# Gates folded into the output weights, q placed by DMA, another order of heads and of first loads, in a fused attention and MLP block

## The chip, the core and the metric

The kernel runs on one core of a Trainium2 chip. The metric is device time in microseconds (us); less is better. The engines named below are PE (matrix products, with PEld for its weight loads), DVE (vector), ACT (activation functions), POOL (GpSimd) and SP, which here only starts DMAs. "Idle" is always the idle time of the engine named.

## What is computed

One transformer block with adaptive layer norm, on 2048 tokens of width 512, 32 heads of 16, an MLP of width 1376, all bfloat16:

```python
mod = (silu(c) @ w_mod).reshape(1, 6, 1, 512)
sa, ca, ga, sb, cb, gb = mod[:, 0], mod[:, 1], mod[:, 2], mod[:, 3], mod[:, 4], mod[:, 5]
h = layernorm(x) * (1 + ca) + sa
q, k, v = heads(h @ wqkv)                       # 32 heads of 16
o = softmax(q @ k.T * 0.25) @ v
x = x + ga * (o @ wo)
h = layernorm(x) * (1 + cb) + sb
x = x + gb * (gelu(h @ w1 + b1) @ w2 + b2)
```

`c` has 512 numbers. The gates `ga` and `gb` are vectors of 512, one number for each output column.

## The kernel before

**A planner writes the order.** The code describes operations (`Op`, with engine, estimated time, dependencies, priority) to a small planner (`Plan`), which simulates the engines and emits the instructions of every engine in the order in which it picks them. The order is fixed when the program is built; on the chip each engine runs its own list from the front, waiting on semaphores. Dependencies given to the planner only shape that order; real waits come from the data.

**Tiling.** Tokens are cut into 4 query blocks of 512 and 16 key tiles of 128; the 32 heads stand as 4 column groups `cc` of 128 columns (8 heads of 16). A *run* is one block with half a column group, 4 heads; there are 32 runs, in the order of `runs` (before: block by block, `u` = 0 to 7). One *unit* is the scores of 128 keys by 512 queries of one head: a matmul on 32 rows of PE (L757). Each head of 16 shares its 32 rows with a neighbour, so q is kept as a tile `qm` of two halves in which the other head's rows are zero.

**Two ways to the exponential.** On the A path ACT takes scores out of PSUM, 3 units and 2 units in turn, with Exp (L806, `pt<-st`). On the D path DVE makes an approximate exponential of 4 units out of five shifted integer conversions: 4 instructions L847 (`ph<-ax`) and 4 L862 (`sh<-ph`). Of the 16 key tiles of a run up to 4 may go to D; the planner decides how many, by the time it thinks each engine has. 32 x 16 x 4 = 2048 units in all; before, 1584 go to ACT and 464 to DVE. PE then multiplies by v (L895).

**The start.** SP issues the loads in one queue: x's first block in four pieces, two pieces of `w_mod` for the first modulation (L480, tiles `blk`), then Wk, Wq, Wv and more of x. ACT's queue loads c (L470) as 128 partitions of 4 numbers. DVE normalises x's first block (L564 statistics, L575), PE makes the modulation columns (L539), transposes the normalised block (L612), DVE and ACT modulate it (L583, L580), then PE projects q, k (L649) and v (L678) for the first column group, and the first scores go to ACT. Blocks 1 to 3 follow the same way, each one's K being needed before ACT can go on past the keys of the blocks before it.

**q.** For every later group of heads (15 of them) `make_q` projects 128 columns and one DVE instruction (L667) reads the PSUM result twice, multiplies by a mask that holds the scale and zero, and writes both halves of `qm`. Four `qm` buffers rotate.

**The tails.** `block_tail` (L1077 on) runs for each block after its heads: PE multiplies by Wo (L1045), DVE multiplies the PSUM result by `ga_bc`, the gate spread over all partitions (L1095, `y<-ax,ga_bc`), and adds x (L1097); a second layer norm, W1, gelu and W2 follow, then again a gate (L1146) and an addition (L1149), and the store. The last block's second half has the same pair in `last_half` (L1203 and L1206, L1250 and L1253).

**GpSimd** computes small powers for the layer norms, scaled copies of v (L694) and the normalised attention output (L947); the last are placed by `beside`, which lays each 0.68 us piece next to a DVE instruction that the planner expects not to share a port with it. SP also carries, for each run, a chain of small DMAs through DRAM that spreads the softmax sums (L926, L928, L936, L941, L957).

Of the kernel before, what the change touches and what calls it, by code (L numbers as in the profile page):

```python
# [53 lines left out]
PEL = 0.24  # L54
# [48 lines left out]
class Plan:  # L103
    SLACK = {"NIL": 0.0, "PE": 0.10, "DVE": 0.05, "ACT": 0.15, "POOL": 0.05, "SP": 0.05}

    def __init__(self, dyn, later):
# [4 lines left out]
        self.bus = 0.0  # L111
# [65 lines left out]
    def commit(self, s, o):  # L177
# [36 lines left out]
        if o.kb:  # L214
            self.bus = max(self.bus, s + o.us + 0.9) + o.kb / 260.0
            o.end = self.bus + 0.7
# [13 lines left out]
    def step(self):  # L230
# [6 lines left out]
        if h is not None:  # L237
            hs = max(self.start(h), self.cool)
            end = hs + h.us + 0.11
            if hs <= nxt and (not pe or pe[0][0] >= end or pe[0][1].kind == "qkD" and hs >= self.cool):  # L240
                self.commit(hs, self.add(h))
                if h.acq is not None:
                    h.acq.free[h.slot] = h.end
                return True
# [5 lines left out]
def kernel(  # L250
# [69 lines left out]
    r_qm = res("qm", 4, [P, 2, QB], BF16)  # L320
# [4 lines left out]
    r_y = res("y", 2, [P, D], BF16)  # L325
# [81 lines left out]
    def dma(fn, deps=(), kb=64, eng="SP", n=1, **k):  # L407
        o = op(eng, fn, 0.45 * n if eng == "SP" else 0.1, deps, **k)
# [9 lines left out]
    def heat():  # L418
        if o_warm.end is None or plan.now > plan.until:
            return None  # L420
        if min(r_ax.free) <= max(plan.now, plan.cool):
# [3 lines left out]
        r = pv_run[0]  # L425
        if r is None or left[r] == 0:
# [10 lines left out]
    plan.heat = heat if True else None  # L437
# [7 lines left out]
    c_bf = const.tile([P, NC], BF16, name="c_bf")  # L445
    ce = const.tile([P, NC], FP32, name="ce")
# [23 lines left out]
    o_c = dma(lambda o: nc.scalar.dma_start(out=c_bf, in_=c.rearrange("o (j p) -> p (o j)", p=P)),  # L470
# [15 lines left out]
    o_wm = {i: load_w(wm_src[:, :, i * D:(i + 1) * D], r_blk, prio=0.1) for i in (0, 1)}  # L486
    o_w = {}
    for n, i in enumerate((1, 0, 2)):
        o_w[i] = load_w(wq_src[:, :, i * D:(i + 1) * D], r_w, prio=(0.2, 0.3, 0.5)[n])
    for b in range(1, NQ):  # L490
        o_x[b] = load_x(b)
        o_x[b].prio = 0.4 if b == 1 else b
# [37 lines left out]
    def silu(o):  # L530
        nc.vector.tensor_scalar(out=ce, in0=ce, scalar1=1.0, scalar2=None, op0=ALU.add)
        nc.vector.reciprocal(out=ce, in_=ce)
        nc.vector.tensor_tensor(out=sc, in0=c_bf, in1=ce, op=ALU.mult)
    o_sc = op("DVE", silu, 0.3, (o_ce,), prio=0.0)

    def mod_mm(ps, n, w, m):
# [4 lines left out]
        if m % 2:  # L541
# [3 lines left out]
    def mod_columns(dst, ws, kind):  # L545
        mm = chain([(lambda ps, n=n, w=w, m=m: mod_mm(ps, n, w[1](), m), 0.36)
# [4 lines left out]
        def out_(o):  # L551
# [3 lines left out]
        return op("DVE", out_, 0.3, (mm,), prio=0.0, rel=(mm,))  # L555
    urgent.add("modA")
    o_mA = mod_columns(modA, [(o_wm[i], lambda i=i: o_wm[i].tile, o_wm[i]) for i in range(2)],
                       "modA")
# [33 lines left out]
    def layer_norm(src, deps, mod, mod_dep, hold_z, alloc_h, engines, ps_res, kind, prio,  # L592
# [3 lines left out]
        st = [op("DVE", lambda o, t=t: stats(ln, t, src(t)), 0.83, (deps[t], ln, after), prio=prio)  # L596
# [9 lines left out]
        if isinstance(ps_res, tuple):  # L606
            for half in range(2):
                def tr(o, half=half):
                    o.ps = o.tile.bitcast(BF16)
                    for j in (2 * half, 2 * half + 1):  # L610
                        for t in range(TPB):
                            nc.tensor.transpose(  # L612
                                out=o.ps[:, (j % 2) * QB + t * P:(j % 2) * QB + (t + 1) * P],
                                in_=z.tile[:, t, j * P:(j + 1) * P], identity=ident)
                one = op("PE", tr, 8 * 0.0705, za + [o_id], lat=PEL, mode=("full", 0), kind=kind,
                         acq=ps_res[half], rel=(z,))
                trs.append(one)
                for j in (2 * half, 2 * half + 1):
# [3 lines left out]
                        0.7, (one, mod_dep, h), prio=0.2, rel=(one,)))  # L622
# [25 lines left out]
    def proj(b, w, cc, kind, acq, after=None):  # L648
# [3 lines left out]
            [w, after] + o_hd[b], kind, acq, (o_h[b], w))  # L652

    def make_k(b, cc, kind, acq, eng, after=None):
        mm = proj(b, o_w[1], cc, kind, acq, after)
        o_k[(cc, b)] = op(eng, lambda o: copy(eng, kT[cc][b], mm.tile[:, 0:QB]), 0.6 if eng == 'DVE' else 0.5, (mm,), prio=0.3,
                          rel=(mm,))

    def make_q(b, cc, kind, acq):
# [6 lines left out]
        else:  # L666
            evs = 2 * [op("DVE", lambda o: nc.vector.tensor_tensor(  # L667
                out=qm.tile, in0=mm.tile[:, 0:QB].unsqueeze(1).to_broadcast([P, 2, QB]),
# [724 lines left out]
```

The softmax here doesn't subtract the row's maximum and nothing guards it: scores larger than these inputs give would overflow.

## Time and profile before

| what | value |
|---|---|
| seven runs | 793.02, 793.47, 794.97, 797.55, 797.68, 798.32, 798.80 us |
| median | 797.55 us |
| profiled execution, one of the seven | 793.47 us |
| its span in the trace | 791.7 us |
| PE, DVE, ACT, POOL busy | 728.6, 737.0, 761.8, 100.4 us |
| L806, Exp on ACT | 634 instructions, 719.5 us |
| DMA over the span | 26.22 MB, mean 33 GB/s |
| first Exp starts / last Exp ends | 17.64 us / 766.18 us |

The busy time of a group counts overlapping instructions once, so the 634 Exps take 719.5 us although one of them is under way for 1309 ns on average: the next starts before the last is quite finished. The 1.8 us between span and run time lie outside the trace.

### The profile page before, as it was taken

What the parts mean: (1) busy time and instruction counts of PE and PEld (TensorE: products, weight loads), DVE (VectorE), ACT (ScalarE), POOL (GpSimd) and SP (SyncE); (2) the same over time, 40 slices, a digit from 0 to 9 for tenths busy, and PEclk for the clock granted to TensorE, in tenths of its full rate; (3) what the DMA queues carried; (4) which work ended last, traced back from release to release, by engine and by line L of the source; (5) the groups of instructions that cost most, each with busy time, mean ns of one, the idle gap of its engine ahead of it and who ended that gap; (6) DMA issues with size and microseconds to landing.
All of it is one profiled execution on the core that took longest, in us unless ns stands there. A gap on an engine that the chain in (4) does not pass through costs nothing.

```text
span 791.7 us, 20215 instructions
## 1 busy us (share of the span) xinstructions
PE 728.6 (92%) x8181; PEld 275.3 (35%) x8260; DVE 737.0 (93%) x1292; ACT 761.8 (96%) x691; POOL 100.4 (13%) x237
## 2 busy tenths in 40 slices
PE   7799998999899899989999899999999899999997
PEld 3433333332232233222222323323234443444454
DVE  6878888999999999989999999999999999999974
ACT  2899999999999999999999999999999999999993
POOL 4612312100001100000001000000000100001100
PEclk8999999999999999999999999999999999999999
DMA  6314000102100000001100000001010000100110
GB/s 212 108 32 108 18 17 16 28 21 72 42 19 16 20 15 17 19 8 30 52 19 16 16 19 3 19 16 32 23 49 19 5 18 17 46 18 17 31 44 27
DMA packets 34199, 26.22 MB, mean 33 GB/s; under 512 B 15005, under 2 KB 29502, under 8 KB 34106
## 3 DMA queue, kind: packets, MB, share of 16 engines
q1 hardware_dynamic: 33578, 24.94, 11.1%
q8 instruction: 64, 1.05, 0.5%
q14 instruction: 29, 0.24, 0.1%
q10 hardware_dynamic: 528, 0.00, 0.0%
HBM read 21.30 MB, written 2.61 MB: 30 GB/s over the span
## 4 chain that ended last, share of the span: by engine, by line
ACT 39%; PE 33%; DVE 15%; issue 12%; DMA 1%; SPq 0%; POOLq 0%; POOL 0%; ACTq 0%; DVEq 0%
ACT pt L806 38%; PE od L895 11%; PE st L757 9%; DVE ph L847 6%; DVE sh L862 5%; PE ax L1051 3%; PE ax L757 2%; PE ax L1114 2%; PE ax L649 1%; DMA blk<-in_w_mod_dram 1%; DVE g L1124 1%; ACT g L1133 1%; PE ax L1045 1%; DVE OD L920 1%; PE t L1051 1%
## 5 line engine op out<-in xcount | busy, mean ns | idle before, releaser
L806 ACT ACTIVATE pt<-st 128x1536 bf16<-128x1536 f32 x634 | 719.5, 1309 | 2.6 <-PE st L757 1.9
L847 DVE TENSOR_SCALAR ph<-ax 128x512 int16<-128x512 f32 x464 | 303.2, 685 | 15.3 <-PE ax L757 13.4
L862 DVE TENSOR_SCALAR sh<-ph 128x2048 int16<-128x2048 int16 x464 | 300.3, 693 | 0.3 <-PE od L895 0.2
L757 PE MATMUL st<-qm,kT 32*128 32x512 bf16 x1584 | 248.0, 382 | 33.6 <-ACT pt L806 25.9
L757 PEld LDWEIGHTS <-kT 32*128 32x128 bf16 x2048 | 83.3, 91 | 247.2 <-issue 235.5
L895 PE MATMUL od<-sh,VX 128*32 128x512 bf16 (+1 forms) x2336 | 164.5, 340 | 4.7 <-DVE sh L862 3.6
L757 PE MATMUL ax<-qm,kT 32*128 32x512 bf16 x464 | 160.9, 379 | 5.4 <-DVE ph L847 2.5
L895 PE MATMUL od<-pt,VEB 128*32 128x512 bf16 (+1 forms) x1976 | 145.0, 340 | 0.7 <-DVE OD L920 0.4
L895 PEld LDWEIGHTS <-VEB 128*32 128x32 bf16 x2560 | 62.2, 96 | 74.5 <-issue 60.2
L895 PEld LDWEIGHTS <-VX 128*32 128x32 bf16 x2336 | 56.9, 95 | 84.2 <-issue 73.5
L947 POOL TENSOR_TENSOR OT<-OD,RB 128x256 bf16<-128x256 f32 x38 | 27.9, 745 | 312.6 <-DVE sh L862 177.8
L895 PE MATMUL od<-ph,VEB 128*32 128x512 bf16 (+1 forms) x584 | 45.6, 338 | 0.3 <-DVE OD L920 0.2
L947 POOL TENSOR_TENSOR OS<-OD,RB 128x256 bf16<-128x256 f32 x24 | 17.2, 726 | 176.9 <-DVE sh L862 172.6
L1114 PE MATMUL ax<-blk,W 128*128 128x512 bf16 (+1 forms) x126 | 36.5, 368 | 2.1 <-issue 1.0
L649 PE MATMUL ax<-blk,w 128*128 128x512 bf16 x95 | 31.9, 391 | 2.8 <-issue 1.0
L694 POOL TENSOR_SCALAR VX<-VEB 128x128 bf16<-128x128 bf16 x64 | 24.1, 376 | 69.6 <-DVE VEB L590 58.0
L1051 PE MATMUL ax<-w,g 128*128 128x512 bf16 x101 | 28.2, 381 | 2.0 <-DVE ph L847 1.5
L1124 DVE TENSOR_SCALAR g<-ax,b1c 128x512 bf16<-128x512 f32 (+1 forms) x37 | 26.3, 715 | 0.3 <-PE ax L1114 0.2
L564 DVE BATCH_NORM_STATS2 ln_s<-xb 128x6 f32<-128x512 bf16 x32 | 21.8, 681 | 0.8 <-DMA xb<-in_A_x_dram 0.7
L1051 PEld LDWEIGHTS <-g 128*128 128x128 bf16 x176 | 14.7, 97 | 22.5 <-issue 9.3
L920 DVE COPY OD<-od 128x512 f32<-128x512 f32 x31 | 21.2, 685 | 0.2
L1114 PEld LDWEIGHTS <-W 128*128 128x128 bf16 x176 | 14.2, 97 | 20.6 <-issue 13.6
(107 smaller groups left out, 368.5 us busy)
## 6 DMA issues: line engine op xcount, KB each, us to landing
RB<-rn SPq DMA_DIRECT2D x124, 64.0 KB
xb<-in_A_x_dram SPq DMA_DIRECT2D x8, 512.0 KB
out_dram<-o SPq DMA_DIRECT2D x16, 128.0 KB
w<-in_A_wqkv_dram SPq DMA_DIRECT2D x3, 512.0 KB
W<-in_B_w_dram SPq DMA_DIRECT2D x1, 1376.0 KB
blk<-in_w_mod_dram SPq DMA_DIRECT2D x2, 512.0 KB
g<-in_w_mod_dram SPq DMA_DIRECT2D x2, 512.0 KB
xb<-in_w_mod_dram SPq DMA_DIRECT2D x2, 512.0 KB
```

The source lines that it names most:

```text
L649: return chain([(lambda ps, j=j: nc.tensor.matmul(out=ps[:, 0:QB], lhsT=w.tile[:, j, cc * P:(cc + 1) * P], rhs=o_h[b].tile[:, j, :], start ...
L694: nc.gpsimd.tensor_scalar(out=v_cols(VX[(t, ph)])[:, 8 * cc:8 * cc + 8, 0:16], in0=v_cols(v_tile(t, 0))[:, 8 * cc:8 * cc + 8, 0:16], scala ...
L757: nc.tensor.matmul(out=o.tile[:, k * QB:(k + 1) * QB], lhsT=kT[cc][kb][rows, ko * P:(ko + 1) * P], rhs=qm.tile[rows, par, :] if hb is None ...
L806: nc.scalar.activation(out=e.tile[:, 0:len(got) * QB], in_=o.tile[:, 0:len(got) * QB], func=ACT.Exp, scale=ESC)
L847: nc.vector.tensor_scalar(out=ph.tile[:, o.row * QB:(o.row + 1) * QB], in0=o.tile, scalar1=PH_B, scalar2=0.0, op0=ALU.add, op1=ALU.max)
L862: sh = op("DVE", lambda o, j=j: nc.vector.tensor_scalar(out=o.tile, in0=first.tile, scalar1=PH_SH[j], scalar2=None, op0=ALU.add), 0.6, es, ...
L895: nc.tensor.matmul(out=o_od[r].tile[32 * i:32 * i + 32, n * HB:n * HB + w], lhsT=v_tile(kt, ph)[:, c0:c0 + 32], rhs=got[i][:, at:at + w], ...
L920: OD = op("DVE", lambda o: nc.vector.tensor_copy(out=o.tile, in_=od.tile), 0.6, (last,), prio=0.0, acq=r_OD, rel=(od,))
L947: two = beside(lambda c: nc.gpsimd.tensor_tensor(out=OT.tile[:, c], in0=OD.tile[:, c], in1=o5.tile[:, c], op=ALU.mult), (OT,), (OD, o5))
L1051: nc.tensor.matmul(out=ps, lhsT=g[:, f, col:col + P], rhs=rhs, start=(f == 0), stop=(f == NF - 1))
L1114: mm = chain([(lambda ps, f=f, j=j: nc.tensor.matmul(out=ps[:, 0:N], lhsT=W1[:, j, f * P:(f + 1) * P], rhs=h.tile[:, j, 0:N], start=(j == ...
L1124: ev.append(op("DVE", lambda o, f=f, mm=mm: nc.vector.tensor_scalar(out=g.tile[:, f, 0:N], in0=mm.tile[:, 0:N], scalar1=b1c[:, f:f + 1], s ...
```

## The change

- **c by rows.** c is loaded as 4 partitions of 128; silu works on that, PE transposes the result (one 128x4 matmul) and ACT copies it to `sc`.
- **First loads.** The two `w_mod` pieces are issued from ACT's queue, the second after the first small Exp; SP issues Wq, Wk, Wv, then x of blocks 1, 2, 3. PE's warm-up matmuls (on zeros) now also use the bank `od`, and the planner no longer spaces them before the first scores. Block 0's transposes come in two parts; its four modulations alternate DVE and ACT; its projections start on each modulated quarter as it comes.
- **Gates.** After `Wo` and `ga_bc` are there, POOL multiplies Wo (and `WoP`, the copy for the last half) by `ga_bc` in place: 12 pieces of 128x256. The same for W2 with `gb_bc`: 22 pieces. The tails then only add: one DVE instruction reads PSUM and x.
- **q.** One DVE instruction scales the projection into a tile `qs`, 128x512; eight DMAs of 16 partitions, issued from SP, place it into `qm`. POOL zeroes three `qm` tiles at the start. The first group keeps the mask.
- **Order of heads.** After block 0's first column group come block 1's first, block 0's second and block 1's second, then the rest as before; the due times of the K and V projections follow.

```diff
-    o_c = ... c.rearrange("o (j p) -> p (o j)", p=P)
+    o_c = ... c.rearrange("o (j p) -> (o j) p", p=P)
...
-    o_wm = {i: load_w(wm_src[:, :, i * D:(i + 1) * D], r_blk, prio=0.1) for i in (0, 1)}
+    o_wm = {i: dma(lambda o, i=i: nc.scalar.dma_start(out=o.tile, in_=wm_src[:, :, i * D:(i + 1) * D]),
+                   eng="ACT", kb=512, acq=r_blk, prio=0.0, gate=lambda i=i: i == 0 or o_ce.end is not None)
+            for i in (0, 1)}
...
-    for n, i in enumerate((1, 0, 2)):
-        o_w[i] = load_w(wq_src[:, :, i * D:(i + 1) * D], r_w, prio=(0.2, 0.3, 0.5)[n])
+    for n, i in enumerate((0, 1, 2)):
+        o_w[i] = load_w(wq_src[:, :, i * D:(i + 1) * D], r_w, (o_x0[2],), prio=(0.2, 0.3, 0.5)[n])
...
+    o_qz = [op("POOL", lambda o, n=n: nc.gpsimd.memset(QM[n], 0.0), 1.0, prio=0.5 + n) for n in range(1, 4)]
...
-            evs = 2 * [op("DVE", lambda o: nc.vector.tensor_tensor(
-                out=qm.tile, in0=mm.tile[:, 0:QB].unsqueeze(1).to_broadcast([P, 2, QB]),
-                in1=qmask.unsqueeze(2).to_broadcast([P, 2, QB]), op=ALU.mult), 1.14, (mm, qm, o_mask),
-                prio=0.3, rel=(mm,))]
+            qs = op("DVE", lambda o: nc.vector.tensor_scalar(
+                out=o.tile, in0=mm.tile[:, 0:QB], scalar1=QSC, scalar2=None, op0=ALU.mult), 0.6, (mm, qm),
+                prio=0.3, acq=r_qs, rel=(mm,))
+
+            def place(o):
+                for i in range(8):
+                    at = slice(16 * i, 16 * i + 16)
+                    nc.sync.dma_start(out=qm.tile[at, i % 2, :], in_=qs.tile[at, :])
+            evs = 2 * [dma(place, [qs] + o_qz, kb=128, n=8, prio=0.4, rel=(qs,))]
...
-    runs = [(b, u) for b in range(NQ) for u in range(8)]
+    early = [(1, 0),(0, 1),(1, 1)]
+    groups = [(0, 0)] + early + [(b, cc) for b in range(NQ) for cc in range(NC) if (b, cc) not in [(0, 0)] + early]
+    runs = [(b, 2 * cc + p) for b, cc in groups[:LAST * NC] for p in range(2)] + [(LAST, u) for u in range(8)]
...
+    def scaled(parts, gate_t, deps):
+        got = []
+        for w in parts:
+            got += beside(lambda c, w=w: nc.gpsimd.tensor_tensor(
+                out=w()[:, c], in0=w()[:, c], in1=gate_t[:, c], op=ALU.mult), deps, prio=2.0)
+        return op("NIL", None, 0.0, got, lat=0.0, prio=0.0)
...
-            m = op("DVE", lambda o, t=t, a=a, y=y: nc.vector.tensor_tensor(
-                out=y.tile, in0=a.tile, in1=ga_bc, op=ALU.mult), 0.6, (y,), prio=0.1, rel=(a,))
-            res_done.append(op("DVE", lambda o, t=t, y=y: nc.vector.tensor_tensor(
-                out=x2.tile[:, t, :], in0=y.tile, in1=xr.tile[:, t, :], op=ALU.add), 0.33,
-                (m, xr), prio=1.5, rel=(y,), port=True))
+            res_done.append(op("DVE", lambda o, t=t, a=a: nc.vector.tensor_tensor(
+                out=x2.tile[:, t, :], in0=a.tile, in1=xr.tile[:, t, :], op=ALU.add), 0.6,
+                (a, xr), prio=0.1, rel=(a,)))
```

The order of the changed program differs from the old one on every engine, since the planner makes it anew. It has, beside what is listed above, 472 units on DVE and 1576 on ACT (315 Exps of three, 315 of two and one of one; before 317, 316 and one).

## The prediction

> **What bounds the kernel now.** I read the page's busy times first, then the busy times by stretch of 50 us, then ACT's timeline at both ends, then the chain of waits.
>
> ```profile
> PE 728.6 (92%) x8181; PEld 275.3 (35%) x8260; DVE 737.0 (93%) x1292; ACT 761.8 (96%) x691; POOL 100.4 (13%) x237
> ```
> ```profile
> 12.00:13.00 1.00, 0.73 (x7) 0.47 (x5) 0.92 (x2) 0.23 (x1) 0.00 (x0) 0.50 1.10 349
> ```
> ```profile
> 20.00:30.00 10.00, 7.43 (x84) 4.24 (x85) 8.25 (x22) 7.88 (x9) 6.51 (x28) 1.00 0.49 160
> ...
> 60.00:110.00 50.00, 47.10 (x498) 18.60 (x505) 42.63 (x75) 50.00 (x45) 14.44 (x32) 1.00 0.20 50
> ...
> 460.00:510.00 50.00, 47.01 (x473) 15.15 (x471) 49.85 (x85) 50.00 (x45) 2.86 (x4) 1.00 0.06 15
> ```
>
> The columns of the last two are stretch, length, then busy us of PE, PEld, DVE, ACT and POOL, PE's granted clock, DMA share, GB/s. All three big engines look full, but only ACT has no gap: from 30 us to its last Exp at 766 us it is busy 50.0 of 50. DVE has gaps (7.4 us between 60 and 110). So the time is: when ACT starts, what ACT has to do, and a tail after 766 us. In the tail PE has the matmuls: it is busy for all but some 0.8 us from 766.2 to 787.7.
>
> ```profile
> 16.57 0.59 ACT L588 CAST kT<-ax 128x512 bf16<-128x512 f32 x1 [2.35 <-PE ax L649]
> 17.64 3.71 ACT L806 ACTIVATE pt<-st 128x1536 bf16<-128x1536 f32 x3 [0.49 <-PE st L757]
> 22.32 3.28 ACT L806 ACTIVATE pt<-st 128x1024 bf16<-128x1024 f32 x3 [0.97 <-PE st L757]
> 25.80 1.45 ACT L580 ACTIVATE blk<-ax,modA 128x512 bf16<-128x512 bf16 x2 [0.20 <-PE ax L612]
> 27.71 0.59 ACT L588 CAST kT<-ax 128x512 bf16<-128x512 f32 x1 [0.46 <-PE ax L649]
> 28.79 4.62 ACT L806 ACTIVATE pt<-st 128x1536 bf16<-128x1536 f32 x4 [0.48 <-PE st L757]
> ```
> ```profile
> 3.06 6.67 DMA blk<-in_w_mod_dram
> ...
> 11.92 1.01 DVE blk L583 x2
> ...
> 14.93 1.61 PE ax L649 x4
> ```
>
> ACT starts Exp at 17.64 us and then waits 0.97 + 0.20 + 0.46 + 0.48 = 2.1 us for block 1's K. The chain (second fence: start, length) says what the start waits for: the second `w_mod` piece lands at 9.73 us, then everything is in series.
>
> **The change, part by part.**
>
> *Less Exp on ACT.* The changed program has 1576 units on ACT instead of 1584. One unit costs 719.5 / 1584 = 0.454 us (group L806), so 8 x 0.454 = **-3.6 us**, all on the engine that sets the time. It is paid by DVE with 16 instructions:
>
> ```profile
> L847 DVE TENSOR_SCALAR ph<-ax 128x512 int16<-128x512 f32 x464 | 303.2, 685 | 15.3 <-PE ax L757 13.4
> L862 DVE TENSOR_SCALAR sh<-ph 128x2048 int16<-128x2048 int16 x464 | 300.3, 693 | 0.3 <-PE od L895 0.2
> ...
> L667 DVE TENSOR_TENSOR qm<-ax,qmask 128x1024 bf16<-128x1024 f32 x15 | 18.3, 1221 | 0.0
> ...
> L1146 DVE TENSOR_TENSOR y<-ax,gb_bc 128x512 bf16<-128x512 f32 x14 | 9.6, 684 | 1.6 <-PE ax L1051 1.6
> ...
> L1149 DVE TENSOR_TENSOR o<-y,xb 128x512 bf16<-128x512 bf16 x14 | 5.8, 418 | 0.0
> ```
>
> 8 x 0.653 + 8 x 0.647 = 10.4 us added. DVE loses the 32 additions from SBUF, 5.8 + 5.7 (L1097) + 0.8 + 0.8 (last half) = 13.1 us, because one addition out of PSUM (taken as the 0.684 of L1146, the same shape from PSUM) does the work of two; and q falls from 1.221 to 0.685 (L847's read of the same PSUM shape), 15 x 0.54 = 8.0. So DVE ends 10.7 us lighter: the price has cover.
>
> *Folding on POOL.* 34 pieces at 0.73 (L947, the same 128x256) are 25 us on an engine that is 13% busy, after the first runs and before block 0's tail. What they can cost is DVE time: a piece outlasts the 0.60 us DVE step it is laid beside (four L847 take 2.5 us) by 0.13, so at most 34 x 0.13 = 4.4 us, at least 0. DVE's gaps of 7.4 us (60 to 110) and 4.0 us (110 to 160) hide it: 0 taken; without them 4.4.
>
> *The start.* From the landing at 9.73 to the first Exp are now 7.91 us. After: 16 modulation matmuls, 2 x 0.36 = 0.7 (the two fillers among them go); modA 0.4 (11.07 to 11.44); two modulations in turn on ACT, beside DVE's, 1.45; transposes are done before, from two parts; the last q matmul and four for k, 0.4 + 1.0 (the 1.0 is the k projection at 17.81 us, at full clock); kT 0.6; scores 0.45; waits between engines 0.1: 5.1 us, **2.8 less**. That is at full clock. The granted clock is 0.50 from 9.5 to 16.3 us now, after 1.65 us of idle PE before 8.31; there the projection of k takes 1.61. If it stays low: 0.55 more for the modulation and 0.9 for q and k, gain 1.4. I take full clock, since 18 fillers ahead of c's transpose and 4 + 4 around the first `w_mod` piece stand in PE's list where it now idles.
> What the sum needs besides is when the second `w_mod` piece lands. It stood third in one queue (1.57 MB with x's block 0). Now it is alone with its twin in ACT's queue, while SP's queue goes on to Wq: if both get equal shares 0.52 MB of Wq come first, 1.5 us at the 349 GB/s of the row above. Against that the first piece is issued at about 1.2 instead of 2.59 us, at most 1.4 earlier. I take 0, as the two nearly cancel: **-2.8**, ends +0.1 and -4.2.
> The Trainium skill speaks against this part (DMA: Bandwidth & Descriptors, "Issuing engines are not separate DMA queues"): all issuers run on the same 16 engines and interleave, so a second issuer saves only issue time. By that rule the landing is later by the 1.5, and this term would be -1.3.
> On the clock it says (TensorE: Matmul & The Clock Gate, "What's actually happening") that about 3.4 us of sustained work lift the half clock and an idle window of that length brings it back; the 0.50 after 9.5 us, and its end at 16.3, fit. By it the term is -2.8 if the fillers close the gap, -1.4 if not.
>
> *The 2.1 us wait for block 1.* Between the first q (14.97) and block 1's modulation (25.36) DVE has 10.4 us of work in a row. The 1.22 of the second q and one 0.85 statistics move behind it, so K can come up to 2.1 earlier, counted from the first Exp. But block 1's x moves behind Wv in the queue, 0.52 MB or 1.5 us later. Ends 0 and -2.1, half taken: **-1.1**. POOL zeroes three tiles, 3 x 0.95 (its 128x1024 memset), from 2.55 to 5.4 us, just before its first power at 5.47: hidden.
>
> *The tail.* The last step is now an addition after a gate:
>
> ```profile
> 787.71 0.69 DVE L1146 TENSOR_TENSOR y<-ax,gb_bc 128x512 bf16<-128x512 f32 x1 [0.51 <-PE ax L1051]
> 788.43 0.42 DVE L1149 TENSOR_TENSOR o<-y,xb 128x512 bf16<-128x512 bf16 x1
> ```
>
> 0.42 goes for certain; earlier pairs only feed PE, whose one gap for DVE there is 0.43 (778.80). **-0.6**, ends -0.4 and -0.9.
>
> *q by DMA.* This is the wait that the change adds. Eight issues at 0.615 (four of the same shape, L957, take 2.46 us) and a landing 1.74 after the last one's start (L926's copy to the next DMA that waits for it): 0.69 + 7 x 0.615 + 1.74 = 6.7 us from the start of the scaling, against 1.2. In the changed program 5 Exps of 719.5 / 634 = 1.135 us lie between scaling and first reader in one group of 15, 6 in four, 7 in two, 9 to 27 in the others. So the nearest readers wait 1.0 and about 0; behind them stands PE's whole list, hence ACT's next scores, but ACT has a second tile of scores filled, about one Exp. The slowest such issue, 1.007, makes it 9.5 us: 3.8, four times 2.7, twice 1.6 late; less 1.1 each, 10 us. **+0.6**, ends 0 and +10. SP's own chain behind them, L926 to L957, is wanted only a run later, 23 us (749 us of Exp stage / 32).
>
> *Order of heads.* K and V of the second group come two runs later; DVE's work only moves. Nothing taken; if it helps, it is in the 8 units.
>
> **Sum.** -3.6 - 2.8 - 1.1 - 0.6 + 0.6 = -7.5: 793.47 becomes 786.0. The profiled execution lies 4.1 below the median, and 4 of 7 runs above 797; nothing here says that the spread goes, so I take the sum off the median: **790.0 us**.
>
> **Rivals.** (1) *The loads only share*: landing 1.5 later, low clock, block 1's x late. Start +0.1, wait 0, and -3.6 - 0.6 + 0.6 + 0.1 = -3.5: 794.0. For it: 349 GB/s already at 12 us. Against: only 131 GB/s between 2 and 3 us, room for a second queue. (2) *q comes late*: placements stand in SP's list behind DMAs that wait (L936 up to 5.7 us for DVE, L957 up to 7.3 for POOL). With 5.7 more, readers wait 5.6, four times 4.5, twice 3.4, once 1.1, together 31 us; in half of the groups 15.5: 790.0 + 15.5 = 805.5, slower than before. It decides from 8 us of such waits in all, where the gain is gone; 12 make it slower by more than 0.5%. For it: SP waits in 216.7 us for L926 alone. Against: those are mostly waits at the head of an empty list. (3) *DVE falls behind*: the 4.4 us of POOL's pieces land where DVE is 49.9 of 50, and PE and ACT wait: -7.5 + 4.4 = -3.1, 794.4.
>
> **Chances.** Forecast 0.58, (1) 0.20, (2) 0.11, (3) 0.11. About 0.5%, 4.0 us, is what a measurement can tell from no change. Faster by more: most of the forecast and a good third of (1) and (3), 0.65; slower (2), 0.10; the rest 0.25. The range: below, start and wait at their ends (-1.4, -1.0) and 4 us if the upper runs vanish, 783.5; above, up to no change, 797.5, which leaves out (2).
>
> **What would show it.** Exps on ACT cost 716 us; the first starts near 15 us, with full clock from 10 us; ACT has about 1 us idle before 30 us and none to 755; PE's wait for `qm` stays under 1 us in all; one DVE instruction after the last matmul. Wrong would be: an ACT row of less than 49.5 of 50, a first Exp after 16.5, PE waiting for a DMA.

## The result, and the profile after

The changed kernel takes 799.18 us (median of 24 runs, 795.55 to 805.98), the kernel before 794.75 us (61 runs, 791.66 to 799.15): a ratio of 1.0057, 95% interval 1.0042 to 1.0072. It is slightly slower, where 790.0 us was forecast.

The profiled execution of the changed kernel took 797.01 us, span 795.2 us, beside 793.47 and 791.7 before. First the busy times, then the stretches shown of before and a worse one near the end (start and end, length, then busy us of PE, PEld, DVE, ACT and POOL, PE's granted clock, DMA share, GB/s).

```profile
PE 727.5 (91%) x8240; PEld 274.4 (35%) x8322; DVE 735.8 (93%) x1276; ACT 760.6 (96%) x689; POOL 124.4 (16%) x274
```
```profile
20.00:30.00 10.00, 7.98 (x82) 3.93 (x80) 9.18 (x24) 7.21 (x9) 6.34 (x26) 1.00 0.18 53
60.00:110.00 50.00, 46.30 (x485) 17.88 (x486) 42.97 (x76) 50.00 (x46) 8.06 (x20) 1.00 0.26 73
...
460.00:510.00 50.00, 46.74 (x466) 14.92 (x463) 46.61 (x79) 48.98 (x44) 2.91 (x4) 1.00 0.09 25
610.00:660.00 50.00, 44.83 (x702) 19.96 (x701) 46.20 (x84) 47.87 (x43) 4.71 (x8) 1.00 0.09 20
```

The totals say nothing: every engine but POOL is less busy than before. The rows do: ACT has 48.98 and 47.87 of 50 us where it had 50.0, and DVE, which bounds nothing by its total, has also become emptier (46.61 where it was 49.85). Something makes both wait. The start and the end of ACT's and DVE's timelines (start, length, engine, line, what; in brackets the idle time before and what ended it):

```profile
14.93 0.59 ACT L604 CAST kT<-ax 128x512 bf16<-128x512 f32 x1 [1.33 <-PE ax L674]
16.01 6.88 ACT L842 ACTIVATE pt<-st 128x1536 bf16<-128x1536 f32 x6 [0.49 <-PE st L793]
24.49 1.45 ACT L596 ACTIVATE blk<-ax,modA 128x512 bf16<-128x512 bf16 x2 [1.59 <-PE ax L633]
26.65 0.59 ACT L604 CAST kT<-ax 128x512 bf16<-128x512 f32 x1 [0.72 <-PE ax L674]
27.72 3.71 ACT L842 ACTIVATE pt<-st 128x1536 bf16<-128x1536 f32 x3 [0.48 <-PE st L793]
```
```profile
791.67 0.69 DVE L1185 TENSOR_TENSOR o<-ax,xb 128x512 bf16<-128x512 f32 x1 [1.66 <-PE ax L1094]
```

The first Exp comes at 16.01 us instead of 17.64; then ACT waits 1.59 + 0.72 + 0.48 = 2.79 us for block 1's K, more than the 2.1 before. One DVE instruction stands behind the last matmul. Summed over the span:

| part of the span | before | after | difference |
|---|---|---|---|
| start to the first Exp | 17.64 | 16.01 | -1.63 |
| ACT's work from first to last Exp | 745.63 | 744.11 | -1.52 |
| ACT idle there, up to 30 us | 2.12 | 2.79 | +0.67 |
| ACT idle there, after 30 us | 0.78 | 7.41 | **+6.63** |
| last Exp to the end | 25.53 | 24.89 | -0.64 |
| span | 791.70 | 795.21 | +3.51 |

The change gains 3.8 us where it was meant to, and loses 7.3 in new gaps of ACT. Who waits is in the view of waits (engine, tile and line, what released it: us in total, times, longest); first before, then after:

```profile
PE od L895 <- DVE sh L862: 3.6, 17, 0.3
...
DVE dc L931 <- DMA dc<-dn: 0.2, 1, 0.2
```
```profile
DVE dc L967 <- DMA dc<-dn: 6.6, 7, 2.2
PE od L931 <- DVE sh L898: 6.1, 24, 1.0
...
PE ax L793 <- DMA qm<-qs: 2.1, 2, 1.2
```

DVE stands 6.6 us, seven times, in front of a reciprocal of 128x16 numbers (L967, 0.25 us each), which waits for a small DMA of the softmax sums. In three of the seven stands (3.7 us) the eight placements of a q were issued between the two transfers that the sums need (out to DRAM, `dn`, and back, `dc`); in two (1.3 us) the first of the two was itself held behind them; in the other two (1.6 us) no placement is near. These transfers are now on the chain that ended last, where the prediction had only the first load:

```profile
2.10 8.04 DMA blk<-in_w_mod_dram
...
523.21 1.82 DMA qm<-qs
...
588.00 3.71 DMA dc<-dn
...
613.49 3.04 DMA dc<-dn
```

And this is how the longest of them comes about. SP's own issues (start, length, line, transfer):

```profile
607.27 0.53 SPq L962 DMA_DIRECT2D dn<-OD  x1
608.47 4.96 SPq L702 DMA_DIRECT2D qm<-qs  x8
613.49 0.58 SPq L964 DMA_DIRECT2D dc<-dn  x1
```
```profile
616.61 0.25 DVE L967 RECIPROCAL dc<-dc 128x16 f32<-128x16 f32 x1 [2.17 <-DMA dc<-dn]
```
```profile
616.48 0.37 PE L793 MATMUL ax<-qm,kT 32*128 32x512 bf16 x1 [1.17 <-DMA qm<-qs]
...
618.26 1.02 ACT L842 ACTIVATE pt<-st 128x1024 bf16<-128x1024 f32 x1 [1.26 <-PE st L793]
```

The sums leave at 607.27. Their second transfer comes next in the chain, but the scaled q was evicted meanwhile and the planner put all eight placements first: 4.96 us in one piece. `dc` is issued only at 613.49 and lands at 616.6. DVE runs its list in order and had reached the reciprocal 2.17 us earlier; behind it stand the conversions that PE waits for (0.52 us at 620.25), and behind PE the scores of ACT. ACT's gap of 1.26 us at 618.26 comes more directly from the other wait on the same placement: PE stood 1.17 us for the q itself, until 616.48. Of the 6.4 us that ACT's gaps of over 0.1 us add up to after 30 us, 3.7 begin within 7 us after a stand, this 1.26 among them.

### The profile page after: what moved, and what is told of

Same layout as the page of the kernel before. It is cut to its first block, busy times and chain, and to the rows that moved or that the text cites. A ratio compares the mean times of both kernels' runs of the same rounds, so it can differ in the third digit from the quotient of the medians.

```text
span 795.2 us, 20495 instructions
## 1 busy us (share of the span) xinstructions
PE 727.5 (91%) x8240; PEld 274.4 (35%) x8322; DVE 735.8 (93%) x1276; ACT 760.6 (96%) x689; POOL 124.4 (16%) x274
## 3 DMA queue, kind: packets, MB, share of 16 engines
q8 instruction: 65, 1.06, 0.6%
## 4 chain that ended last, share of the span: by engine, by line
ACT 36%; PE 31%; DVE 18%; issue 11%; DMA 3%; SPq 1%; POOL 0%; ACTq 0%; DVEq 0%
ACT pt L842 33%; PE od L931 11%; PE st L793 9%; DVE sh L898 7%; DVE ph L883 7%; PE ax L1094 2%; PE ax L1154 2%; PE ax L793 2%; ACT g L1173 1%; DMA dc<-dn 1%; DVE OD L956 1%; DMA blk<-in_w_mod_dram 1%; PE ax L674 1%; DVE ln_s L580 1%; PE ax L711 1%
## 5 line engine op out<-in xcount | busy, mean ns | idle before, releaser
L842 ACT ACTIVATE pt<-st 128x1536 bf16<-128x1536 f32 (+1 forms) x631 | 717.7, 1294 | 8.2 <-PE st L793 3.5
L883 DVE TENSOR_SCALAR ph<-ax 128x512 int16<-128x512 f32 x472 | 309.2, 684 | 21.2 <-PE ax L793 19.2
L898 DVE TENSOR_SCALAR sh<-ph 128x2048 int16<-128x2048 int16 x472 | 310.7, 700 | 0.8 <-PE od L931 0.4
L931 PE MATMUL od<-sh,VX 128*32 128x512 bf16 (+1 forms) x2384 | 167.6, 341 | 7.3 <-DVE sh L898 6.1
L793 PE MATMUL ax<-qm,kT 32*128 32x512 bf16 x472 | 163.4, 379 | 8.1 <-DVE ph L883 4.2
L793 PEld LDWEIGHTS <-kT 32*128 32x128 bf16 x2048 | 79.8, 91 | 240.9 <-issue 230.3
L931 PE MATMUL od<-pt,VEB 128*32 128x512 bf16 (+1 forms) x1964 | 146.6, 340 | 1.0 <-issue 0.5
L931 PEld LDWEIGHTS <-VX 128*32 128x32 bf16 x2384 | 60.0, 95 | 89.2 <-issue 80.0
L931 PEld LDWEIGHTS <-VEB 128*32 128x32 bf16 x2560 | 64.0, 96 | 76.2 <-issue 61.7
L674 PE MATMUL ax<-blk,w 128*128 128x512 bf16 x93 | 30.1, 382 | 4.0 <-issue 1.3
```

Source lines behind the costliest of these rows:

```text
L674: return chain([(lambda ps, j=j: nc.tensor.matmul(out=ps[:, 0:QB], lhsT=w.tile[:, j, cc * P:(cc + 1) * P], rhs=o_h[b].tile[:, j, :], start ...
L793: nc.tensor.matmul(out=o.tile[:, k * QB:(k + 1) * QB], lhsT=kT[cc][kb][rows, ko * P:(ko + 1) * P], rhs=qm.tile[rows, par, :] if hb is None ...
L842: nc.scalar.activation(out=e.tile[:, 0:len(got) * QB], in_=o.tile[:, 0:len(got) * QB], func=ACT.Exp, scale=ESC)
L883: nc.vector.tensor_scalar(out=ph.tile[:, o.row * QB:(o.row + 1) * QB], in0=o.tile, scalar1=PH_B, scalar2=0.0, op0=ALU.add, op1=ALU.max)
L898: sh = op("DVE", lambda o, j=j: nc.vector.tensor_scalar(out=o.tile, in0=first.tile, scalar1=PH_SH[j], scalar2=None, op0=ALU.add), 0.6, es, ...
L931: nc.tensor.matmul(out=o_od[r].tile[32 * i:32 * i + 32, n * HB:n * HB + w], lhsT=v_tile(kt, ph)[:, c0:c0 + 32], rhs=got[i][:, at:at + w], ...
```

## The experiments

Theory 1: the placements hold up SP, and through L967 DVE, PE and ACT. Theory 2: POOL's folding slows DVE. Theory 3: the new order of heads makes the plan tight. Theory 4: short stretches of half clock. All kernels ran against the kernel before on the same chip; "idle" is ACT's from 30 us to the last Exp, "stand" DVE's wait at the reciprocal, "half" the time at half clock from the first to the last Exp, each in the kernel's own profiled execution. That is one execution: the changed kernel's, at 797.01 us and a mean granted clock of 0.997, is one of its faster ones (its 25 executions average 0.9908), so its 3.4 us of half clock is less than is usual for it. The versions "start + placement", with and without the order, hold the scaled q in one buffer instead of two.

| kernel | units on DVE | median us | ratio, 95% interval | idle | stand | half |
|---|---|---|---|---|---|---|
| *VectorE masks q* | | | | | | |
| before | 464 | 794.75 | 1 | 0.8 | 0.2 | 0 |
| before, null edit | 460 | 799.24 | 1.0057 (1.0036, 1.0079) | 4.1 | 1.9 | 10.2 |
| before + folding | 464 | 796.36 | 1.0024 (1.0004, 1.0044) | 5.1 | 0.0 | 17.3 |
| start | 468 | **792.44** | 0.9974 (0.9958, 0.9991) | 1.6 | 1.1 | 0 |
| start, null edit | 460 | 801.44 | 1.0081 (1.0052, 1.0110) | 5.5 | 1.0 | 10.2 |
| start + order | 460 | 797.44 | 1.0030 (1.0008, 1.0051) | 5.1 | 0.5 | 17.1 |
| start + folding | 460 | 800.14 | 1.0055 (1.0034, 1.0076) | 5.1 | 0.0 | 10.2 |
| start + folding + order | 464 | 797.85 | 1.0032 (1.0010, 1.0054) | 3.1 | 0.5 | 3.4 |
| *q placed by DMA* | | | | | | |
| after (all four) | 472 | 799.18 | 1.0057 (1.0042, 1.0072) | 7.4 | 6.6 | 3.4 |
| after, null edit | 464 | 812.27 | 1.0214 (1.0196, 1.0233) | 17.9 | 10.1 | 30.7 |
| before + placement | 464 | 810.31 | 1.0203 (1.0166, 1.0241) | 14.7 | 7.6 | 17.1 |
| start + placement | 464 | 808.36 | 1.0166 (1.0139, 1.0193) | 11.5 | 6.4 | 17.1 |
| start + placement + order | 468 | 813.22 | 1.0236 (1.0206, 1.0266) | 12.9 | 8.3 | 17.1 |
| start + placement + folding | 464 | 812.55 | 1.0210 (1.0175, 1.0244) | 17.5 | 8.3 | 30.7 |
| after, q asked for earlier | 464 | 799.95 | 1.0063 (1.0040, 1.0086) | 9.4 | 8.6 | 17.1 |
| after, placement in four steps | 468 | 804.79 | 1.0122 (1.0090, 1.0155) | 16.3 | 1.8 | 20.5 |
| after, placement's measured cost told | 468 | 796.29 | 1.0027 (1.0005, 1.0048) | 5.4 | 1.0 | 13.7 |
| *after, its order kept* | | | | | | |
| reciprocal on POOL | 472 | 797.44 | 1.0032 (1.0017, 1.0048) | 9.6 | 0 | 10.2 |
| no folding | 472 | 801.19 | 1.0066 (1.0041, 1.0092) | 13.2 | 6.6 | 23.9 |
| VectorE masks q | 472 | 805.66 | 1.0122 (1.0095, 1.0149) | 15.4 | 1.6 | 27.3 |

### The parts by themselves

**The changed kernel with the old masking of q.** 

```diff
-            qs = op("DVE", ... scalar1=QSC ...)
-            evs = 2 * [dma(place, [qs] + o_qz, kb=128, n=8, prio=0.4, rel=(qs,))]
+            evs = 2 * [op("DVE", ... in1=qmask ... op=ALU.mult), 1.14, (mm, qm, o_mask), prio=0.3, rel=(mm,))]
```


> The changed kernel with q made as before (one L667-like DVE instruction, no placement). If the placement's DMAs on SP cause the new gaps of ACT (6.4 us between 30 and 755 us in the changed kernel): those gaps fall under 1.5 us, DVE's waits at the reciprocal of the softmax sums (6.6 us) nearly vanish, and with the start 1.6 earlier and the tail 0.6 shorter the time is about 792.5, ratio 0.997. If GpSimd's folding or the order of heads causes them: gaps stay at 5 us or more, ratio 1.005 or above.

Idle fell from 7.4 to 3.1 us and the stand to 0.5, as theory 1 says, but the median only by 1.3. This version has 8 units fewer on DVE, 3.6 us more of Exps by the prediction's price of a unit, so the two effects stand against each other.

**The changed kernel, the planner told 0.62 us for each placement.**

```diff
-            evs = 2 * [dma(place, [qs] + o_qz, kb=128, n=8, prio=0.4, rel=(qs,))]
+            evs = 2 * [dma(place, [qs] + o_qz, kb=128, n=11, prio=0.4, rel=(qs,))]
```


> The changed kernel, the planner told 4.95 us for the eight placement DMAs instead of 3.6 (the trace has 0.6 us for each). If the lateness against the plan is what hurts, ACT's gaps after 30 us at least halve (under 3.2 us) and the ratio falls to about 1.001. If SP is simply too busy, or the cause lies elsewhere, gaps and ratio stay: 1.005.

The stand goes, with the same transfers on the chip. This line is the group of the reciprocals in that kernel (engine, line, operation, count, busy us, mean ns, idle time before them and what ended it):

```profile
L967 DVE RECIPROCAL dc<-dc 128x16 f32<-128x16 f32 x31 | 7.6, 245 | 1.0 <-DMA dc<-dn 1.0
```

Told how long SP is taken, the planner makes an order in which DVE no longer comes to the reciprocal ahead of its transfer. The time, 796.29 us, is 2.9 less; as the order is another one, not all of that need be the stand (see the null edits).

**The kernel before with the placement alone**, and **with the folded gates alone** (each the part of the diff above, nothing else).

> The kernel before with nothing changed but q placed by DMA. Placement as the cause: gaps of 4 to 6 us on ACT after 30 us, DVE waits at the reciprocal, nothing gained at the start, ratio 1.005 to 1.008. Another cause: ratio 0.999 to 1.001 and ACT without gaps after 30 us, as before.

> The kernel before with nothing changed but the gates folded by GpSimd. If GpSimd's 34 pieces hold up DVE: ACT has gaps of 3 us or more, ratio 1.003 or above. If they are hidden: the tail is 0.6 shorter and the rest the same, ratio 0.999.

Placement alone costs 16 us, folding alone 2. The first is twelve times what the changed kernel showed when placement was taken out of it (1.3 us): the parts don't add.

### Undoing one part, keeping one part

```diff
 placement in four steps:
-                for i in range(8):
-                    ... nc.sync.dma_start(out=qm.tile[at, i % 2, :], in_=qs.tile[at, :])
+                two = [dma(... two of the eight ..., [qs] + o_qz, kb=32, n=2.75, prio=0.4 + 0.1 * p, rel=(qs,)) ...]
 old order of heads:
-    early = [(1, 0),(0, 1),(1, 1)]
+    early = []
```


> The changed kernel, but each placement of q is four steps of two transfers instead of one step of eight, each told to the planner at 1.24 us, so that the transfers of the normalisation (L964 to L977 in the changed kernel) can be issued between them; the even half, which is read first, goes first. 468 units on VectorE (472 in the changed kernel), so 4 x 0.454 = 1.8 us more of Exps on ScalarE. Theory 1 (the eight issues, some 5 us in one piece on SP, hold up the chain behind the row sums): VectorE's wait at the reciprocal falls from 6.6 us to under 1.5, TensorE's wait for q from 2.1 to under 0.5, ScalarE's idle time after 30 us from 6.4 us to 3 or less; median 795.5 to 797.5 against 799.18 of the changed kernel. Theory 2 (GpSimd's folding slows VectorE): idle time after 30 us stays over 5 us, median 799 to 801. Theory 4 (short stretches of half clock, about 1 us each): the median still stands 1 to 3 us over the fastest execution.

> The changed kernel with the heads in the order of the kernel before; q still placed by transfers, the gates still folded. 464 units on VectorE. Theory 1 (placement alone): as many gaps as in the changed kernel, 5 to 8 us after 30 us, and 8 x 0.454 = 3.6 us more of Exps: median 800 to 803. Theory 3 (the order of heads makes the plan tight where block 1 is prepared): gaps after 30 us fall under 3 us and the median to 798 or less. If, as in the kernel before with q by transfers alone (14.5 us of gaps), the old order asks for q at worse moments, gaps are 10 us or more and the median is 804 or more.

> The changed kernel without the placement of q (VectorE masks q as before) and with the old order of heads: the new start and the folded gates are left. 460 units on VectorE, 4 fewer than the kernel before: +1.8 us of Exps. Theory 1: idle time after 30 us under 2.5 us; with the first Exp near 15.2 us (it was so in the version without placement) and the tail at 24.9 the span is 791.7 + 1.8 - 2.4 - 0.6 + 1 to 2 of gaps = 791.5 to 793; median 794 to 797. Theory 2 (folding holds up VectorE): gaps near 150 to 400 us, where GpSimd folds, of 3 us or more, median 797 or more. Theory 3 (new order costs): median at least 1 us under the 797.85 of the version that has the new order.

> The kernel before with the new start alone (c by rows, loads in two queues, the warming matmuls, split transposes): no folded gates, no placement, old order of heads. 468 units on VectorE, 4 more than before: -1.8 us of Exps. If the start is a gain of its own: first Exp at 15.2 to 16.0 us (17.65 before), idle time after 30 us under 1.5 us, span 788 to 790.5, median 790.5 to 793 against 794 to 794.75 before. If the time won at the start is given back (warming matmuls move the stretches of half clock into the Exps): idle time after 30 us 2 us or more, median 793.5 to 796.

The four steps did what they were for, the stand fell to 1.8 us, but then the chain went first and q came late: PE waited 4.2 us for it. In this order SP served one at the cost of the other; the version with the measured cost told shows an order with neither wait (1.0 us of stand, none of PE for q). The new start alone is the only version faster than the kernel before, by 0.26%. The old order was slower than the new one both times, by 13.4 us with placement and by 2.3 without; that is not what theory 3 says.

### The rest of the combinations

> The kernel before with the new start and the new order of heads; no folded gates, no placement of q. 460 units on VectorE against 468 of the new start alone: +3.6 us of Exps by the plan. The wait for block 1 (1.94 us with the new start and the old order) should fall. If the order gains what it seemed to with folded gates (800.14 to 797.85 us): 790 to 792. If the plan's fewer units cost what they say and the wait is all it gains: 792.44 + 3.6 - 1 to 2 = 794 to 795.

> The kernel before with the new start and q placed by eight transfers (one buffer for the scaled q instead of two); no folded gates, old order of heads. If the placement costs with the old order what it cost twice already (793.97 to 810.31, 800.14 to 812.55): 12 to 16 us over the new start alone, 804 to 809, with 8 us or more of idle time after 30 us. If it needs folded gates or the old start for that: under 798.

> The changed kernel without the folded gates: new start, new order, q by eight transfers (one buffer for the scaled q). 468 units on VectorE, 4 fewer than the changed kernel: +1.8 us of Exps. If the folded gates are what cost the changed kernel its gain (they cost 2.4 us in the kernel before and 7.7 beside the new start): 793 to 796 against 799.18. If the placement is the whole cost: 799 to 802.

> The changed kernel with each q asked for 16 steps of the plan (half a run, some 12 us) earlier, nothing else changed; 464 units on VectorE against 472: +3.6 us of Exps. Placement takes about 5 us on SP and lands some 7 us after the eviction, and q was wanted about 8 us after it. If q's lateness and its meeting the normalisation at a run's end are the cause: TensorE waits for q under 0.3 us (2.1), VectorE at the reciprocal under 3 us (6.6), idle time after 30 us under 3 us (6.4); median 797 to 799.5. If the placement still meets the normalisation, idle time stays at 5 us or more and the median is 801 to 804.

```diff
-            due(32 + APR * (first_run(q_made[0]) - 1) - 32)
+            due(32 + APR * (first_run(q_made[0]) - 1) - 48)
```

The diff is that of the last. Without folding the changed kernel is 14 us slower, not faster; the new order costs 5 us without folding (with or without placement) and gains 2 or 13 with it. No sum of fixed prices gives that. Every variant is planned anew, and the plan itself had to be tested.

### The same order, one thing altered

These keep the changed kernel's plan and alter only what the planned step emits.

```diff
 reciprocal on POOL:
-        o3 = op("DVE", lambda o: nc.vector.reciprocal(out=o2.tile, in_=o2.tile), 0.2, (o2,),
+        o3 = op("DVE", lambda o: nc.gpsimd.tensor_tensor(out=o2.tile, in0=o2.tile, in1=mone, op=ALU.pow), 0.2, (o2,),
 no folding:
-            got += beside(lambda c, w=w: nc.gpsimd.tensor_tensor(...), deps, prio=2.0)
+            got += beside(lambda c, w=w: None, deps, prio=2.0)
 VectorE masks q:
-            qs = op("DVE", lambda o: nc.vector.tensor_scalar(... scalar1=QSC ...), 0.6, ...)
+            qs = op("DVE", lambda o: nc.vector.tensor_tensor(out=qm.tile, ... in1=qmask ...), 0.6, ...)
```


> The changed kernel with the same plan (472 units), but the reciprocal of the row sums is taken by GpSimd (power -1) instead of VectorE, at the same place of the plan: VectorE no longer stands at it while the row sums' transfer waits behind the placement on SP. If that stand is the cause: VectorE's 6.6 us wait is gone, ScalarE's idle time after 30 us falls from 7.4 us (all gaps counted) to 4 or less, median 795 to 797 against 799.18. If the late chain costs through something else (the output of the heads, buffers, q itself): idle time 6 us or more, median 798.5 to 800.5.

With POOL standing at the transfer in DVE's place, the median falls by 1.7 us (the intervals overlap at their ends). More than the stand is altered: POOL takes 3.0 us longer for the numbers, and what follows them comes later. At the places where the stands were, ACT's gaps nearly go: 3.7 us in the changed kernel, 0.9 here (at 620.17). In these two executions, at one and the same order, the stand does reach ACT. Yet the idle time of the profiled execution, expected to fall to 4 us or less, rose to 9.6; 3.2 us of it lie in its stretches of half clock or within 1 us after them. The gain goes with the clock: over all executions the mean granted clock is 0.9944 against 0.9908, and within the changed kernel's 25 executions (the profiled one among them) 0.01 of clock is worth 4.6 us, so 0.0036 x 460 = 1.7 us.

> The changed kernel with the same plan, but GpSimd's multiplications of Wo and W2 by the gates are left out (so the gates are not applied at all), 38 of 0.67 us. If the folding slows VectorE (the 128x2048 shifts took 700 ns here, 688 to 693 in kernels without folding, 458 x 10 ns = 4.6 us): the shifts fall to 693 or less, idle time after 30 us falls by 2 to 4 us, median 795 to 797.5. If the folding costs nothing at a fixed plan: idle time 6.5 to 8 us, median 798.5 to 800.

The pieces left out are 34, not 38. The shifts (L898) fell from 700 to 692 ns as expected, and the time did not: theory 2 falls. The folding is hidden, as forecast.

> The changed kernel with the same plan (472 units), but VectorE writes the masked q itself at the place of the scaling (1.22 us instead of 0.68, 15 times: 8 us more on VectorE, which the plan doesn't know), nothing is placed by transfers, and GpSimd's zeroing of the q tiles at the start is left out. If the placement is the cause: waits at the reciprocal under 1 us, for q none, idle time after 30 us 4 us or less; without the zeroing the addition of the silu falls from 1.45 us to about 0.2 and the first Exp comes at 15.2 instead of 16.0; span 790 to 792.5, median 792 to 795. If the plan is the cause, or VectorE's 8 us count: idle time after 30 us 6 us or more, median 797 or more.

This doesn't settle the cause, as two things changed at once: the placement's waits went (stand 1.6 us, no wait for q), and DVE got 8 us of work that the plan doesn't know. Together they cost 6.5 us. It fits that an order is narrow and holds for the durations it was made with, but the run doesn't separate the two.

### Null edits

One cost told to the planner is 0.01 us larger; nothing else in the kernel's text changes. The order does, and with it the split of the units: DVE gets 4 fewer in the kernel before, 8 fewer in the other two, by the price of a unit 1.8 and 3.6 us more of Exps.

```diff
-        OD = op("DVE", lambda o: nc.vector.tensor_copy(out=o.tile, in_=od.tile), 0.6, (last,),
+        OD = op("DVE", lambda o: nc.vector.tensor_copy(out=o.tile, in_=od.tile), 0.61, (last,),
```


> The kernel before, but the planner is told 0.61 us instead of 0.60 for the copy of the head outputs; every operation is the same, the order differs, 460 units on VectorE instead of 464: +1.8 us of Exps by the plan. If a plan drawn anew is worth only its units: 794 to 797. If the kernel before holds an unusually good order, which any edit loses: 797 to 802, with 3 us or more of idle time after 30 us and stretches of half clock. If neither: within 0.2% of the kernel before.

> The changed kernel with the same null edit (0.61 us told for the copy of the head outputs instead of 0.60): same operations, another order, 464 units on VectorE instead of 472 (+3.6 us of Exps). If the changed kernel's time is an ordinary draw of its order: 797 to 805. If, as in the three other kernels that place q by transfers with an order of their own, an ordinary draw loses more: 805 to 813.

> The new start alone with the same null edit: same operations, another order, 460 units on VectorE instead of 468 (+3.6 us of Exps). If the 2 us won against the kernel before belong to the start and not to a lucky order: at least 2 us under the null edit of the kernel before (799.24), 794 to 797.5. If the order decides: 798 to 802.

The null edit costs the kernel before 4.6 us (0.57%, as much as the whole change), the new start 9.0, the changed kernel 13.1. The units explain 1.8, 3.6 and 3.6 us of that. All three held an order better than the next one. In the null edit of the changed kernel the stand is:

```profile
L967 DVE RECIPROCAL dc<-dc 128x16 f32<-128x16 f32 x31 | 7.6, 246 | 10.3 <-DMA dc<-dn 10.1
```

So a difference of 5 us between two single kernels of the table is not the price of a part. Groups are better: the eight kernels in which VectorE masks q have a mean ratio of 1.0032 (0.9974 to 1.0081), the seven in which eight transfers in one piece are told at 3.6 us have 1.0164 (1.0057 to 1.0236). The placement costs about 1.3%, some 10 us, on an ordinary order; the stand is 6.4 to 10.1 us in all seven and at most 1.9 in the eight. Five pairs differ by the placement, its buffers and the plan made anew alone: it adds 0.020 to the ratio of the kernel before, 0.019 beside the start, 0.021 beside start and order, 0.016 beside start and folding, and only 0.003 beside all three. The changed kernel is the best of its seven, the kernel before the second best of its eight.

### The clock

Why do a few us of standing cost 10? In the version that asks for q earlier one stand can be followed (columns as in the stretches above; then SP, DVE and ACT):

```profile
589.60:593.00 3.40, 3.40 (x73) 1.79 (x73) 3.30 (x7) 3.36 (x3) 0.00 (x0) 1.00 0.30 66
593.00:596.40 3.40, 1.70 (x31) 0.78 (x32) 0.64 (x2) 3.40 (x4) 0.00 (x0) 1.00 0.34 112
596.40:603.30 6.90, 6.21 (x58) 1.99 (x61) 5.73 (x11) 3.39 (x4) 0.00 (x0) 0.51 0.14 39
```
```profile
587.85 2.48 SPq L702 DMA_DIRECT2D qm<-qs  x4
590.42 0.53 SPq L962 DMA_DIRECT2D dn<-OD  x1
```
```profile
596.23 0.25 DVE L967 RECIPROCAL dc<-dc 128x16 f32<-128x16 f32 x1 [2.76 <-DMA dc<-dn]
...
598.40 1.45 ACT L842 ACTIVATE pt<-st 128x1536 bf16<-128x1536 f32 x1 [1.88 <-PE st L793]
...
602.51 1.45 ACT L842 ACTIVATE pt<-st 128x1536 bf16<-128x1536 f32 x1 [1.46 <-PE ax L793]
```

DVE stands 2.76 us. The sums were ready at 587.89 and left at 590.42, behind a placement; their second transfer then took 4.1 us beside a 512 KB load of x. PE is busy for half of that stretch (1.70 of 3.40), and for the next 6.9 us its clock is half: ACT is busy for 3.39 of 6.90. Most of the loss comes after the wait has ended; how much of it is the clock, and how much the engines' taking up their lists again, no run separates. In the twenty traces the clock went to half 63 times inside the Exp stage. In the 3.4 us before, PE was busy for 31 to 95% (median 71); of the stretches of that length with full clock behind them 95% had 80% or more, though some had as little as 56%. The mean clock of an execution sorts its time: of the changed kernel's executions the nine at 0.995 or more took 795.55 to 798.03 us, the seven at 0.987 or less 801.10 to 805.98. This part is a correlation; no run changed the clock alone.

## Why the prediction was wrong, step by step

- **Less Exp on ACT, -3.6**: too large. ACT's work fell by 1.52. The Exps are 719.5 us before and 717.7 after, 0.4554 us a unit instead of 0.454. An Exp of three units adds 1.35 us when the next follows at once and takes 1.45 when it starts after a gap (1.45 in the lines of the section on the clock), and the changed kernel has 20 more Exps after a gap. Each gap costs some 0.1 us more than its length.
- **DVE 10.7 us lighter**: it became 1.2 us lighter (737.0 to 735.8). The scaled q (-8.0) and the additions (-13.0) came as priced. The 8 more units cost 16.5 us instead of 10.4, as the shifts take 700 ns instead of 693, and the start costs 3.5 more.
- **The start, -2.8**: right in kind, it measured -1.63. PE's clock was full from 5.2 us, as taken. The second `w_mod` piece landed at 10.14 (2.10 + 8.04 in the chain) instead of the 9.73 taken, 0.4 late. From there to the first Exp it took 5.87 us, not 5.1. What the sum had wrong here is "transposes are done before, from two parts": all sixteen stand in PE's list behind the modulation's matmuls.

```profile
10.18 0.96 DVE L591 TENSOR_SCALAR z<-xb,mv,rs 128x512 bf16<-128x512 bf16 x2 [0.61 <-POOL rs L587]
10.19 0.55 PE L556 MATMUL ax<-sc,blk 128*128 128x1 bf16 x16 [0.71 <-DMA blk<-in_w_mod_dram]
...
10.60 1.16 PE L633 MATMUL st<-ident,z 128*128 128x128 bf16 x16
...
11.58 0.99 DVE L599 TENSOR_SCALAR blk<-st,modA 128x512 bf16<-128x512 bf16 x2 [0.17 <-PE st L633]
```

  The projections of q and k took 1.90 us on the chain (12.99 to 14.89) where 1.4 was priced. A second path ends at the same time. The zeroing of the q tiles was called hidden, but the cover was checked on POOL alone: while POOL zeroes, DVE's addition for silu (4x128) takes 1.45 us instead of 0.18, x's statistics stand behind it, and the last normalisation (L591) ends at 11.14 instead of some 10.1. Six other versions in which that normalisation decides start their first Exp 4.86 or 4.87 us after it; two in which the landing decides, the start alone (9.39, first Exp 15.28) and the reciprocal on POOL (9.71, 15.47), start it 5.89 and 5.76 after that. Both paths give 15.9 to 16.0 here, so the zeroing cost at most about 0.1 us beside this landing. The start with the new order zeroes nothing and starts its Exps at 16.11, after a landing at 9.96.
  The Trainium skill's rule on queues that was weighed there (DMA: Bandwidth & Descriptors, "Issuing engines are not separate DMA queues") gave -1.3 for the start; the piece landed 0.4 us later, not 1.5. That is one execution: in the sixteen versions with the new start it landed between 8.0 and 10.1 us, in the four with the old one between 9.4 and 10.35.
  The prediction's "fit" for the clock was too quick: in the kernel before PE was busy for 1.51 of the 3.41 us ahead of the half clock at 9.46, and no idle stretch there was longer than 1.65 us.
- **The wait for block 1, -1.1**: wrong sign, +0.67. K came 1.06 us earlier (27.71 to 26.65), the first Exp 1.63: the wait counts from the Exp.
- **The tail, -0.6**: right, -0.64.
- **Folding 0**: right; leaving it out at the same order gained nothing.
- **Order of heads 0**: not to be told from the plan: -13.4, -2.3, +4.9 and +5.0 us in four pairs.
- **q by DMA, +0.6 (0 to +10)**: this is the step that failed, in one sentence: "SP's own chain behind them, L926 to L957, is wanted only a run later, 23 us". The end of the chain is; but its reciprocal is an instruction in DVE's list, and DVE cannot pass it. The readers of q, on which the working spent its care, waited 2.1 us; the reciprocal waited 6.6, 5.0 of it with a placement of q in the way. Rival 2 named SP's queue and the slower side, but priced the readers (31 us) and not the chain. Its 805.5 was too high for the changed kernel; of the six other versions that place q in one piece at the same told cost, five took 808 to 813.
- **The sum's base**: the -7.5 was taken off a median of seven executions, 797.55; the 61 executions have 794.75. Against that base the change was forecast at -7.5 and measured +4.4. And the sum priced the parts as if the order around them stayed as good. Null edits of 4.6 to 13.1 us show that the orders of both kernels are far better than the next, so a few us could not be forecast from the parts. How much of the 4.4 us is the placement and how much the plan stays open: taking the stand away at the same order gives 1.7, and the remaining 2.7 is within what one order differs from another.

Of the signs named beforehand, the Exps (717.7, not 716), the first Exp (16.01, under the limit of 16.5) and the tail held or nearly; ACT's row under 49.5 of 50 and PE waiting for a DMA showed the fault.

The version that beats both is the new start alone, 792.44 us; since its null edit takes 801.44, this is the gain of that order too, not of the start by itself.

## What to carry to other kernels

Where a step is moved to a queue that other chains use, follow each of those chains to the engine that waits for it in order: an idle-looking small DMA can hold a full engine. Where a planner or scheduler makes the order anew, build a null edit first and measure it; a part is worth only what exceeds that. Tell a planner the measured cost of an issue: with 0.62 us instead of 0.45 the stand fell from 6.6 to 1.0 us here.

## What the runs showed of the hardware

- PE's clock fell to half without an idle stretch of 3.4 us. The Trainium skill (TensorE: Matmul & The Clock Gate, "HAM oscillation — how this bites in real kernels") gives as the abstract rule that no gap be longer than about 3.4 us. By that rule alone the clock would have stayed full here, where 0.48 us of idle in the stretch before was followed by half clock; the measurement decides. In the changed kernel:

```profile
124.70:128.10 3.40, 2.92 (x37) 1.33 (x37) 3.38 (x6) 3.40 (x4) 2.00 (x4) 1.00 0.46 147
128.10:131.50 3.40, 3.40 (x34) 0.99 (x35) 2.53 (x7) 2.98 (x4) 1.30 (x2) 0.50 0.04 7
```
- DVE's addition of 4x128 fp32 numbers takes 0.18 us in the six versions with the new start in which POOL zeroes nothing beside it. In the ten in which POOL zeroes three bfloat16 tiles of 128x1024 at the same time, it takes 0.46 to 0.73 us (eight) or 1.42 and 1.45 (two), and it ends 0.06 to 0.08 us after the end of the second zeroing or, in the two, of the third.
- POOL's power -1 of 128x16 fp32 numbers takes 3.25 us, DVE's reciprocal of the same 0.25:

```profile
L968 POOL TENSOR_TENSOR dc<-dc,mone 128x16 f32<-128x16 f32 x31 | 100.6, 3246 | 258.1 <-DMA dc<-dn 243.4 <-issue 14.7
```
